# Gate and value products of two units by seven block products for eight, in a kernel of chunk-selected attention and a gated feed-forward

## The chip, the cores and the metric

The kernel runs on one core of a Trainium2 chip. The metric is the device time in microseconds. A core has five engines with a queue each that run side by side and wait for each other by semaphores: TensorE (PE, matmuls, written to the eight banks of PSUM; its weight loads are shown as PEld), VectorE (DVE), ScalarE (ACT), GpSimd (POOL) and SyncE (SP, which here issues most DMA transfers). Each queue is worked off in order.

## The reference

The inputs are q, k and v of 4 batches, 8 heads, 768 positions and 64 dimensions in float32. Keys are seen in 24 chunks of 32. For each query an upper bound of its score in each chunk is formed from the chunk's smallest and largest keys, and the six chunks with the largest bounds are kept. Attention runs over the kept chunks under a causal mask. Its output, with the heads side by side, is a matrix x of 3072 x 512, which goes through a gated feed-forward:

```
ub = sum(max(q * k_min, q * k_max))              # per query and chunk, -1e9 where not causal
sel = the 6 chunks with the largest ub
attn = softmax(where(sel and causal, scale * q @ k.T, -1e9))
x = (attn @ v), heads side by side               # 3072 x 512
out = (sigmoid(x @ w_gate) * (x @ w_val)) @ w_out   # 512 -> 1536 -> 512
```

## The kernel before

The 3072 rows are cut into eight units of 384 (three blocks of 128 positions each). Unit 0 holds first blocks, where nothing has to be selected; units 1 to 7 hold the others. The unit list names them `u0` to `u7`.

For each unit the keys and queries are turned and cast (`prepare`, `keys_wide`, `keys_blocks`, `turn_queries`), then `choose` makes the bounds (`ub`, TensorE), turns them (`ubn`, VectorE), takes the eight largest (`mx`), compares (`ap`), turns the result back (`apt`) and copies it as a mask beside the queries (`hqm`). `attend` makes scores (`sc`, TensorE, line L1064), exponentials (`exp`, ScalarE, L1075), the causal cut (`cm`, GpSimd, L1081), the products with v (`pv`, TensorE, L1097), and scales and turns the result (`rz`, `x`, `xps`, `xT`; L1114 to L1124 and the copies at L575 and L577). So `xT` of a unit is the turned 512 x 384 input of its feed-forward, as four slices of 128 x 384 in float16.

`ffn` (L1131 and after) works on one unit. For each of the 12 blocks `fb` of 128 hidden columns it makes the gate product `g` (four matmuls of 128 x 128 weights with 128 x 384 inputs, added up in one PSUM bank; L1147), `tanh` of half of it on ScalarE (L1155), the value product `v` (four matmuls, L1147), and on VectorE `hg` = (tanh + 1) * v (L1159); the factor 1/2 is put in at the end. Then `o` multiplies the 12 `hg` with w_out for each of the three row blocks, in three parts `o0`, `o1`, `o2` of four matmuls (L1172), `osb` copies the bank (L1181), and `out` stores it.

The weights w_gate, w_val and w_out come by nine transfers that GpSimd issues (`wg0` to `wo2`, L719 to L725); SP issues the loads of q, k and v and the stores.

No operation is emitted where it stands in the code. Each is added to a `Plan` with its engines, its inputs and outputs, its buffers and a priority. Buffers come in kinds with a number of slots (`ps` are the eight PSUM banks). `Plan.order` then walks through all operations with a cost model, and picks at each step an operation, an engine and buffer slots; a list of nudges and a list of landing times of the transfers steer it. The result is the order in which the operations are emitted, and so the order of each engine's queue.

Of the kernel before, what the change touches and what calls it, by code (L numbers as in the profile page):

```python
# [17 lines left out]
HOP = {PE: 60, ACT: 40, DVE: 40, POOL: 70, SP: 30}  # L18
FAR = float("inf")
STEP, PHASE, AWAKE = 3413.0, 300.0, 0.58  # L20
SHARED = {128: (0.145, 0.95), 256: (0.173, 0.90), 512: (0.22, 0.83), 768: (0.29, 0.78), 2048: (0.5, 0.5)}
SENT, LANDED = {SP: 700, POOL: 2700}, 1100
# [12 lines left out]
class Op:  # L35
    def __init__(self, name, engines, emit, prio, dma, rows, port):
        self.name, self.engines, self.emit, self.prio, self.dma = name, engines, emit, prio, dma
        self.rows, self.port = rows, port
        self.deps = []
        self.bufs = []  # L40
        self.start = self.done = self.engine = None


class Clock:


    def __init__(self):
        self.full = {}
        self.busy = {}

    def rate(self, t):
        w = int((t - PHASE) // STEP)
        if w not in self.full:
            self.full[w] = self.busy.get(w - 1, 0.0) >= AWAKE * STEP
        return self.full[w]

    def took(self, s, busy):
        t, left = s, busy
        while left > 1e-6:
            slow = 1.0 if self.rate(t) else 1.9  # L60
            w = int((t - PHASE) // STEP)
            edge = PHASE + (w + 1) * STEP
            step = min(left * slow, edge - t)
            self.busy[w] = self.busy.get(w, 0.0) + step
            left -= step / slow
            t += step
            if edge - t < 1e-6:
                t = edge
        return t - s


class Plan:

# [36 lines left out]
    def walk(self, land, prio=None, script=None, slow=1.0):  # L110

        free = {e: 0.0 for e in HOP}
        slots = {k: [[0.0, None] for _ in range(n)] for k, n in self.slots.items()}
        line = {SP: 0.0, POOL: 0.0}
        port = {DVE: 0.0, POOL: 0.0}
        flight = []
        clock = Clock()
        left, until, seen = {}, {}, {}
        out = []

        def inputs(op, e):
            t = 0.0
            for d, raw in op.deps:
                if raw is None:
                    t = max(t, d.start)
                elif d.dma is None and d.engine == e:
                    if raw and e != PE:
                        t = max(t, d.done + 25)
                else:
                    t = max(t, d.done + HOP[e])  # L130
            for b in op.bufs:
                if b.kind == "ps":
                    for (other, r), done in seen.get(b, {}).items():
                        if other != e and r in op.rows:
                            t = max(t, done + HOP[e])
            if e == POOL:
                t = max(t, port[DVE])
            elif e == DVE and op.port:
                t = max(t, port[POOL])
            return t  # L140

        def room(op):
            t = 0.0
            if script is not None:
                for b in op.bufs:
                    if b not in left:
                        t = max(t, slots[b.kind][b.slot][0])
                return t
            need = {}
            for b in op.bufs:  # L150
# [3 lines left out]
            for (kind, cat), bs in need.items():  # L154
                kinds[kind] = kinds.get(kind, 0) + len(bs)
                if (kind, cat) in self.caps:
                    mine = sorted(s[0] for s in slots[kind] if s[1] is not None and s[1].cat == cat)
                    over = len(mine) + len(bs) - self.caps[kind, cat]
                    if over > 0:
                        t = max(t, mine[over - 1])  # L160
# [143 lines left out]
NUDGES = """  # L304
# [1007 lines left out]
```

## Time and profile before

| what | value |
|---|---|
| time, median of 3 runs | 293.85 us (293.5 to 294.12) |
| span of the profiled execution | 292.8 us |
| timed median less that span | 1.05 us |
| PE busy | 277.3 us, 95% |
| DVE busy | 188.2 us, 64% |
| ACT busy | 195.5 us, 67% |
| POOL busy | 91.8 us, 31% |
| granted TensorE clock, mean | 0.988 |
| `g` and `v` matmuls (L1147), all units | 384 each, 79.1 and 78.8 us busy |
| `hg` on DVE (L1159) | 96, 545 ns mean |
| `tanh` on ACT (L1155) | 96, 496 ns mean |

The profile is one execution of the program; its span reaches from the first to the last instruction. "Busy" is the union of an engine's instructions, so a mean duration times a count is more than the busy time where instructions overlap. The windows view gives the busy time of each engine in a stretch, with the number of instructions in brackets and the granted TensorE clock. The waits view tells for each engine what ended its idle time: microseconds in total, times, the longest.

### The profile page before, as it was taken

To read this page: it belongs to the slowest core of one execution; us is meant where nothing else is said; L and a number is where in the kernel's file an instruction comes from. 1 tells how busy PE (TensorE), PEld (TensorE's weight loads), DVE (VectorE), ACT (ScalarE), POOL (GpSimd) and SP (SyncE) were. 2 spreads that over 40 slices of the span, in tenths; PEclk is the share of its full clock that TensorE was granted. 3 is DMA by queue.
4 is the path that set the end of the run, shared out by engine and by line. 5 is a ranking of instruction groups with operands and counts; after the bars stand their busy time and mean duration, and the time that the engine had idled before them with its cause. 6 is when DMAs were issued, how large, how long until landed. Compare 5 with 4: busy or idle time off the path is not lost.

```text
span 292.8 us, 6981 instructions
## 1 busy us (share of the span) xinstructions
PE 277.3 (95%) x2668; PEld 177.3 (61%) x2668; DVE 188.2 (64%) x560; ACT 195.5 (67%) x399; POOL 91.8 (31%) x162
## 2 busy tenths in 40 slices
PE   2769998999999999999999999999999999999995
PEld 2545655767664566556666668676566556655653
DVE  8276883996999289999899999654134124423420
ACT  7575747977984879458889998877464466332321
POOL 5663304934652337013336864212000011000000
PEclk9977999999999999999999999999999999999999
DMA  7999999999968999499995300001100020002002
GB/s 164 213 251 223 197 199 241 216 143 172 182 101 90 201 168 191 82 209 169 152 211 124 113 3 3 0 2 39 72 2 1 36 74 0 2 36 74 0 2 107
DMA packets 123377, 32.69 MB, mean 112 GB/s; under 512 B 111440, under 2 KB 120400, under 8 KB 123344
## 3 DMA queue, kind: packets, MB, share of 16 engines
q1 hardware_dynamic: 118592, 27.53, 53.3%
q0 software_dynamic: 4752, 4.72, 9.5%
q8 instruction: 21, 0.34, 0.5%
q14 instruction: 12, 0.10, 0.1%
HBM read 30.67 MB, written 6.29 MB: 126 GB/s over the span
## 4 chain that ended last, share of the span: by engine, by line
PE 73%; DMA 12%; DVE 6%; SPq 3%; POOL 2%; issue 1%; ACT 0%; DVEq 0%; ACTq 0%
PE o_u L1172 20%; PE g_u L1147 16%; PE v_u L1147 16%; PE sc_u L1064 10%; DMA wo<-in_moe_w_out_dram 8%; PE pv_u L1097 6%; SPq L743 2%; DMA kq_u<-in_k_dram 2%; PE ube_u L1003 2%; DMA k<-in_k_dram 2%; PE xps_u L1124 2%; DVE kcr L788 1%; DVE kt L954 1%; DVE kx L788 1%; SPq L738 1%
## 5 line engine op out<-in xcount | busy, mean ns | idle before, releaser
L1075 ACT ACTIVATE att_u<-sc_u 128x512 f16<-128x512 f32 (+3 forms) x184 | 88.1, 550 | 14.3 <-PE sc_u L1064 13.6
L1159 DVE SCALAR_TENSOR_TENSOR hg_u<-gate_u,v_u 128x384 f16<-128x384 f16 x96 | 51.9, 545 | 53.6 <-PE v_u L1147 36.7
L1147 PE MATMUL g_u<-xT_u,wg 128*128 128x384 f16 x384 | 79.1, 329 | 0.0
L1147 PE MATMUL v_u<-xT_u,wv 128*128 128x384 f16 x384 | 78.8, 328 | 0.2 <-DMA wv<-in_moe_w_val_dram 0.2
L1155 ACT ACTIVATE gate_u<-g_u 128x384 f16<-128x384 f32 x96 | 47.6, 496 | 38.6 <-DVE hg_u L1159 21.5
L1172 PE MATMUL o_u<-wo,hg_u 128*128 128x512 f16 (+1 forms) x288 | 67.4, 377 | 1.3 <-DMA wo<-in_moe_w_out_dram 1.3
L1081 POOL TENSOR_SCALAR_AFFINE_SELECT att_u<-att_u 128x384 f16<-128x384 f16 (+1 forms) x56 | 28.2, 509 | 102.5 <-ACT att_u L1075 101.7
L1147 PEld LDWEIGHTS <-wv 128*128 128x128 f16 x384 | 36.7, 98 | 23.2 <-DMA wv<-in_moe_w_val_dram 0.6
L1147 PEld LDWEIGHTS <-wg 128*128 128x128 f16 x384 | 36.5, 99 | 21.7 <-issue 1.5
L1172 PEld LDWEIGHTS <-hg_u 128*128 128x128 f16 x300 | 27.9, 98 | 28.5 <-issue 1.7
L1181 ACT ACTIVATE osb_u<-o_u 128x512 f32<-128x512 f32 (+1 forms) x20 | 12.0, 598 | 26.1 <-PE o_u L1172 24.4
L1097 PEld LDWEIGHTS <-att_u 128*128 128x128 f16 x640 | 25.5, 98 | 4.7
L1097 PE MATMUL pv_u<-v,att_u 128*128 128x65 f16 x640 | 27.9, 193 | 0.0
L1064 PE MATMUL sc_u<-hqo,hko 128*128 128x128 f16 (+2 forms) x220 | 27.8, 243 | 0.1
L1064 PE MATMUL sc_u<-hqe,hke 128*128 128x128 f16 (+2 forms) x220 | 27.1, 243 | 0.2 <-ACT att_u L1075 0.2
L1064 PEld LDWEIGHTS <-hke 128*128 128x128 f16 x220 | 16.8, 98 | 5.7 <-issue 1.2
L1064 PEld LDWEIGHTS <-hko 128*128 128x128 f16 x220 | 16.2, 98 | 4.8 <-issue 0.2
L780 POOL CAST v<-v 128x512 f16<-128x512 f32 x23 | 13.9, 617 | 16.8 <-DMA v<-in_v_dram 16.6
L577 DVE COPY xT_u<-xps_u 128x384 f16<-128x384 f16 (+1 forms) x17 | 5.8, 339 | 14.4 <-PE xps_u L1124 14.3
L1116 DVE TENSOR_TENSOR x_u<-pv_u,rz_u 128x384 f16<-128x384 f32 (+1 forms) x28 | 14.5, 524 | 0.4
L1026 DVE MAX8 mx_u<-ubn_u 128x8 f32<-128x8 f32 (+16 forms) x152 | 12.4, 158 | 0.1
L788 DVE TRANSPOSE_TENSOR_REDUCE kcr<-k 128x24 f32<-128x768 f32 x12 | 11.3, 944 | 0.3 <-DMA k<-in_k_dram 0.3
(121 smaller groups left out, 306.1 us busy)
## 6 DMA issues: line engine op xcount, KB each, us to landing
v<-in_v_dram SPq DMA_DIRECT2D x23, 256.0 KB, 5.4
out_dram<-osb_u SPq DMA_DIRECT2D x23, 256.0 KB, 2.5
k<-in_k_dram SPq DMA_DIRECT2D x12, 384.0 KB, 6.0
q<-in_q_dram SPq DMA_DIRECT2D x12, 384.0 KB, 6.5
wg<-in_moe_w_gate_dram POOLq DMA_DIRECT2D x3, 512.0 KB, 9.5
wv<-in_moe_w_val_dram POOLq DMA_DIRECT2D x3, 512.0 KB, 11.5
wo<-in_moe_w_out_dram POOLq DMA_DIRECT2D x3, 512.0 KB, 21.9
kf<-in_k_dram SPq DMA_DIRECT2D x8, 128.0 KB, 3.9
```

The source lines that it names most:

```text
L780: plan.add(f"v16_{b}_{ib}", {POOL: pool(H * D)}, lambda e: nc.gpsimd.tensor_copy(v16[b % 2][:, ib, :, 0:D], at(t)), reads=[t], writes=[("v ...
L788: plan.add(f"kx{m}_{name}_{p}", {DVE: dve(size)}, lambda e, m=m, op=op: nc.vector.tensor_reduce(out=outs[m](), in_=src(), op=op, axis=AX.X ...
L1026: nc.vector.max(at(mx)[:, e_, j, :], at(ubn)[:, e_, j, 0:max(8, u.seen[j])])
L1064: nc.tensor.matmul(at(t)[:, o:o + 128 * m], hk[b % 2][e_][:, p, 128 * jb:128 * jb + 128], hq[u.side][e_][:, p, 128 * x:128 * (x + m)], sta ...
L1075: plan.add(f"exp_{u.name}_{h}_{y}", {ACT: act(n)}, lambda e, t=t, att=att, b0=b0, n=n: nc.scalar.activation(at(att)[:, b0:b0 + n], at(t), ...
L1081: nc.gpsimd.affine_select(out=dv, in_=dv, compare_op=ALU.is_ge, fill=0.0, base=0, pattern=[[0, u.m], [1, 128]], channel_multiplier=-1)
L1097: nc.tensor.matmul(at(pv)[:, last, x, :], at(att)[:, c:c + 128], v16[b % 2][:, jb, h, :], start=(jb == 0), stop=(jb == ib))
L1116: plan.add(f"x_{u.name}_{p}", {DVE: dve(u.t)}, lambda e: nc.vector.tensor_tensor(at(x_).rearrange("p a (e d) -> p e a d", e=2), at(pv)[:, ...
L1147: nc.tensor.matmul(at(t), w16[:, c, 128 * fb:128 * fb + 128], at(u.xt)[:, c, :], start=(c == 0), stop=(c == 3))
L1155: plan.add(f"tanh_{u.name}_{fb}", {ACT: act(T)}, lambda e, g=g, gate=gate: nc.scalar.activation(at(gate), at(g), AF.Tanh, scale=0.5), read ...
L1159: plan.add(f"hg_{u.name}_{fb}", {DVE: dve(T)}, lambda e, w_=w_, gate=gate, hg=hg: nc.vector.scalar_tensor_tensor(at(hg), at(gate), 1.0, at ...
L1172: nc.tensor.matmul(at(o), at(hgs[fc])[:, 128 * tb:128 * tb + 128], wo16[:, fc, lo:hi], start=(fc == 0), stop=(fc == NFB - 1))
```

## The change

For units 5 and 6, `ffn` is replaced by `ffn_pair`, which takes both at once. The weights of gate and of value are seen as 2 x 2 blocks (halves of the 512 inputs by halves of the 1536 hidden columns), the two units' inputs as 2 x 2 blocks (halves of the inputs by unit). The 2 x 2 product of blocks takes seven products for eight, with sums of blocks in their place. For each of six pairs of hidden blocks `f` and `f + 6`, and for gate and value each, there are seven products `P1` to `P7` of two matmuls, in three PSUM banks (`su`, `sq`, `sr`), three copies `E0`, `E1`, `E3` of partial results to SBUF in float32 and three adds `C0`, `C1`, `C3`. `tanh` and `hg` then read three of the four results from SBUF and one from PSUM.

The sums of weight blocks (`Sg0` to `Sg3`, `Sv0` to `Sv3`) are made once, 128 x 1536 in float16, the sums of inputs (`T0` to `T3`) once, 128 x 768 in float16.

The projection of all units is now made by `project_out`, with the same matmuls; for the pair the order in which the 12 parts are added is another. Unit 7's `xT` takes a slot of the kind `qf`, since units 5 and 6 hold both slots of `xt` at once.

The cost model, the nudges and the landing times are gone. `ORDER` is a table of 1782 words, one for each operation in the order of emission, with an engine where it is not the first one allowed and with the buffer slots. The table is another order for all units, not for units 5 and 6 alone. In it the selection and the first scores of unit 7 come ahead of those of unit 6, and units 5 and 6 reach their products together, before unit 7's first.

```diff
-    def walk(self, land, prio=None, script=None, slow=1.0):
...
+    def order(self):
+        ops = {op.name: op for op in self.ops}
+        out = []
+        for word in ORDER.split():
+            name, _, slots = word.partition(":")
+            name, _, engine = name.partition("@")
+            op = ops.pop(name)
+            op.engine = engine or next(iter(op.engines))
+            fresh = [b for b in op.bufs if b.slot is None]
+            for b, slot in zip(fresh, slots.split(",") if slots else (), strict=True):
+                b.slot = int(slot)
             out.append(op)
...
+ORDER = """
+vf1_3:0 kf0_0:0 v10 ap0 vf1_2:1 ident hq1 kf1_0 epat0:0 vf1_1:2 qf0_0:1 ident16 v11 hq0 epat kcr0 qf1_0 ap1 kcr1
...
+qf0_u7_2 v16_3_4 exp_u5_0_1 Sv0@DVE:0 g_u4_0:2,0,12 qm_u7_2@ACT sc_u5_2_2:0,3 osb_u3_2@DVE cm_u5_1 sc_u5_0_2:5
...
+    def mixed(w16, name, key, prio, raw):
...
+        for i, x, op, y, need in ((0, a21, ALU.add, a22, []), (1, s(0), ALU.subtract, a11, [(t, 0)]),
+                                  (2, a11, ALU.subtract, a21, []), (3, a12, ALU.subtract, s(1), [(t, 1)])):
+            op = plan.add(f"S{name}{i}", {POOL: pool(n), DVE: dve(n, 2)}, lambda e, i=i, x=x, op=op, y=y: (
+                nc.vector if e == DVE else nc.gpsimd).tensor_tensor(at(t)[:, i], x(), y(), op),
...
+    def ffn_pair(ua, ub_, base, span):
...
+        for i, x, op, y, need in ((0, b12, ALU.subtract, b11, ka[0:2] + kb[0:2]), (1, b22, ALU.subtract, tt(0), kb[2:4] + [(ts, 0)]),
+                                  (2, b22, ALU.subtract, b12, kb), (3, b21, ALU.subtract, tt(1), ka[2:4] + [(ts, 1)])):
...
+                op = mul(1, u_, True)
...
+                keep_(0, u_)
+                mul(2, q_, True)
+                add(0, q_)
+                mul(5, r_, True)
+                keep_(3, r_)
+                use(0)
+                mul(6, u_, False)
+                keep_(1, u_)
+                mul(3, r_, False)
+                add(1, r_)
+                use(1)
+                mul(7, u_, False)
+                add(3, u_)
+                use(3)
+                mul(4, u_, False)
+                use(2)
...
-    ffn(units[5], 6.0, 0.95)
...
+    mix = {"g": mixed(wg16, "g", "wg", 5.4, k3), "v": mixed(wv16, "v", "wv", 5.6, q3)}
     attend(units[6], 6.0)
-    ffn(units[6], 7.0, 0.95)
+    ffn_pair(units[5], units[6], 6.4, 1.6)
```

Here `mul` is a product of two matmuls, `keep_` a copy `E`, `add` an add `C`, and `use` a `tanh` for the gate or an `hg` for the value. So in the bank `su` the products 1, 6, 7 and 4 are added up one after the other, and what stands in it is read (`E0`, `E1`, `C3`) before the next product adds to it.

## The prediction

> **What bounds the kernel now.** I read the page's shares first, then the windows, the waits of TensorE, and the timeline of the stretch that the change replaces.
>
> ```profile
> span 292.8 us, 6981 instructions
> ...
> PE 277.3 (95%) x2668; PEld 177.3 (61%) x2668; DVE 188.2 (64%) x560; ACT 195.5 (67%) x399; POOL 91.8 (31%) x162
> ```
>
> ```profile
> core 0: us, PE busy (x) PEld busy (x) DVE busy (x) ACT busy (x) POOL busy (x), PEclk, DMA share, GB/s
> 0.00:20.00 20.00, 10.24 (x83) 7.54 (x83) 12.29 (x33) 13.88 (x22) 11.75 (x26) 0.96 1.05 202
> 20.00:40.00 20.00, 19.85 (x140) 11.62 (x139) 14.59 (x50) 11.49 (x26) 7.13 (x12) 0.87 1.21 215
> ...
> 160.00:180.00 20.00, 20.00 (x316) 13.64 (x314) 18.66 (x77) 18.41 (x37) 13.37 (x23) 1.00 0.19 54
> 180.00:200.00 20.00, 20.00 (x237) 14.57 (x235) 13.30 (x40) 15.85 (x34) 5.08 (x9) 1.00 0.01 2
> 200.00:220.00 20.00, 20.00 (x166) 12.16 (x164) 5.47 (x13) 12.01 (x26) 2.57 (x5) 1.00 0.11 41
> 220.00:240.00 20.00, 20.00 (x146) 11.62 (x144) 4.99 (x10) 9.72 (x19) 1.04 (x2) 1.00 0.11 41
> 240.00:260.00 20.00, 20.00 (x192) 12.88 (x190) 8.48 (x18) 9.14 (x20) 1.01 (x2) 1.00 0.00 1
> ```
>
> From 100 us to 280 us TensorE is busy all the time at clock 1.00. Its 12.3 us of idleness lie before 100 us (the five windows there hold 87.7 of 100 us). VectorE is nearly full from 120 to 180 us (18.7 to 19.0 of 20) and a quarter full after 200 us, where the products of units 5 and 6 stand. A busy TensorE need not be at its peak, so I look at the spacing.
>
> ```profile
> 216.43 0.81 PE L1147 MATMUL g_u<-xT_u,wg 128*128 128x384 f16 x4
> ...
> 217.08 0.81 PE L1147 MATMUL v_u<-xT_u,wv 128*128 128x384 f16 x4
> ...
> 217.73 0.81 PE L1147 MATMUL g_u<-xT_u,wg 128*128 128x384 f16 x4
> ```
>
> Four matmuls start every 0.65 us, 0.1625 us each; nothing else stands between them. So a matmul taken away here is worth 0.1625 us, as long as TensorE still finds its inputs ready.
>
> **What is removed.** Units 5 and 6 now take 2 x 12 x 2 products of four matmuls: 48 x 0.65 = 31.2 us. The change takes 2 x 6 x 7 products of two matmuls: 84 x 0.325 = 27.3 us. It saves 24 matmuls (and 24 weight loads, which lie beside them: PEld is 61% busy), 3.9 us of TensorE. All other TensorE work is the same, in another order.
>
> **What is added, and its price.** VectorE gets 36 adds `C`, 8 copies `E`, 7 of the weight sums `S` (128x1536) and 4 activation sums `T` (128x768). ScalarE gets 28 copies `E`, GpSimd one `S`. The 24 `tanh` and 24 `hg` stay.
>
> ```profile
> 184.61 0.56 DVE L1116 TENSOR_TENSOR x_u<-pv_u,rz_u 128x384 f16<-128x384 f32 x1
> 185.08 0.54 DVE L1159 SCALAR_TENSOR_TENSOR hg_u<-gate_u,v_u 128x384 f16<-128x384 f16 x1
> 185.54 0.57 DVE L1037 STREAM_TRANSPOSE apt_u<-ap 128x384 f16<-128x384 f16 x1
> ```
>
> Back to back, a 128x384 operation of VectorE takes 0.47 us of it; alone, it lasts 0.55. That is the price of `C`, `E` and `hg`. No row shows a 16-bit sum of two SBUF tensors. Nearest from below: the f16 copy of 64x1536 at 0.55. From above, four times 0.47 = 1.88 for 1536 elements at one per cycle. I take a middle row, 16-bit data that come through one port: the f16 copy `xT_u` takes 0.286 for 256 and 0.358 for 384 elements, 0.072 per 128 more, so 1.0 us for `S` and 0.57 for `T`.
>
> ```profile
> L577 DVE COPY xT_u<-xps_u x17: 248/358/358, 56.1 to 265.4; 128x384 f16<-128x384 f16 x15, 128x256 f16<-128x256 f16 x2
> L577 DVE COPY xT_u<-xpsf x6: 280/286/292, 16.5 to 69.6; 128x256 f16<-128x256 f16 x6
> L577 DVE COPY hke<-epat x3: 547/547/555, 5.7 to 6.6; 64x1536 f16<-64x1536 f16 x3
> ```
>
> The Trainium skill, VectorE: DVE Perf Modes, section "The perf-mode tier table", says that such a sum of two 16-bit SBUF tensors runs at two elements per cycle; by its breakdown an estimate for `S` would be 0.95 us, and the sum below would stand. At the one element per cycle of this case's two-source rows it would go to the slower rival.
>
> **Where it lies: three stretches of the table.** I add the operations of each stretch by their row prices.
>
> (1) From `Sv0` to `o0_u4_0`, where the eight `S` are put among unit 4's products and the selection of units 7 and 6. TensorE: 28.5 us. VectorE without `S`: 12 `hg` and 4 `x` at 0.47 (7.5), 4 each of `ubn` and `apt` at 0.5 (4.0), 4 `mx` at 1.0 (4.0), 4 `ap` at 0.4 (1.6), 7 `hqm` at 0.36 (2.5), small ones 3: 22.6. With 7 `S` at 1.0: 29.6, 1 us more than TensorE has. With the lower price 26.5, with the upper 35.8. This is the part of the trace where VectorE is full already, and it is in order: `hqm` of unit 6 is queued behind all `S`, and unit 6's scores behind it. I take 0.5 us lost, half of the excess, because the last of the stretch's operations are not all waited for at once.
>
> Another cost is in this stretch. `ap` reads two SBUF tensors, and lasts 0.84 us where GpSimd worked beside it (its cast at 172.32 lasted 0.82), 0.46 where it did not:
>
> ```profile
> 172.61 0.84 DVE L1031 TENSOR_TENSOR ap<-ubn_u,mx_u 128x288 f16<-128x288 f32 x1
> 175.78 0.46 DVE L1031 TENSOR_TENSOR ap<-ubn_u,mx_u 128x288 f16<-128x288 f32 x1
> ```
>
> `S` reads two as well. GpSimd works some 9 of 28 us here, so a third of the 7 meet it: 7/3 x 0.4 = 0.9 us at most. It is within the excess that I only half count, and goes to the range. The Trainium skill, SBUF — State Buffer, section "Who interferes with whom", has this as a rule against the change: a sum with both inputs in SBUF waits for a GpSimd instruction that reads SBUF; were all seven hit, it would be 2.8 us of VectorE for the 0.9, and the sum up to 1.9 us worse.
>
> (2) From `P1g_u5u6_0` to `g_u7_0`: TensorE 18.9 us (51 half products, 16.6, and 2.3 of unit 7's attention). VectorE: 22 `C`, 9 `hg`, 5 `E`, 2 `x`, 38 x 0.47 + 0.5 = 18.4 us, 97%. If each operation took its lone 0.55: 21.4, 2.5 more than TensorE has. Within one group the bank `su` goes to and fro: four products and three reads of it, 4 x 0.325 + 3 x (0.5 + some 0.25 of matmul end and hand-over) = 3.5 us, against 2.3 us that TensorE works for the group. So two or three groups must interleave, as the table has them, and what covers one group's wait is another's products. I take 1.4 us lost, between 0 and 2.5: no engine that is 97% full and waits at each step keeps the other one full.
>
> (3) From `g_u7_0` to `g_u7_4`: TensorE 19.8 us, VectorE 35 x 0.47 = 16.5 (lone: 19.3). No loss taken. Before (2), VectorE has 4 of 16.7 us to do, then the `T`: 4 x 0.57 ahead of `P1g`, beside 4.4 us of TensorE: covered; at 0.94 each it would stand out by nothing to 1 us. ScalarE stays under 80% in (2) and (3). After `g_u7_4` come 28.5 us of TensorE with 4 us of VectorE.
>
> **The front.** Its operations are the same, their order isn't. The second key half is now SP's second transfer and no longer the third (one step, 0.55 us earlier; the first transpose waits for it), `hkf1` and `hkp111` (0.6 and 1.5 us) stand ahead of `wg0` on GpSimd, `vf_0` goes from fifth to fourteenth on SP, and `vc_2` moves to GpSimd. All nine weight loads keep their order, and the last one, `wo2`, still holds unit 0's projection:
>
> ```profile
> PE o_u L1172 <- DMA wo<-in_moe_w_out_dram: 1.3, 1, 1.3
> ```
>
> TensorE has 28.0 us of work ahead of that wait in both orders, so `wo2` ties the two together: without it up to 1.3 us could go, and a start later by 1.5 would shift everything. I take 0, with -1.3 to +1.5 in the range.
>
> **Sum.** The profiled execution has a span of 292.8 us; the timed median is 293.85, 1.05 more. 292.8 - 3.9 + 0.5 + 1.4 = 290.8, and with the 1.05: **291.9 us**.
>
> **Rivals.** *VectorE becomes the bound* (slower). Place: stretch (1). If `S` runs at one element per cycle (1.88), VectorE has 35.8 us to TensorE's 28.5; 7.3 lost for 0.5, so 298.7. It decides from the point where the losses pass 3.9 us: `S` over some 1.2 us each, with 1.4 lost in (2). Half of it: 295.0. For it: VectorE's 18.7 of 20 us there, and the two-source rows. Against: the 16-bit rows. *The work is hidden fully*: nothing lost in (1) and (2), 290.0; with the front's 1.3 gained, 288.7. For it: in 120 to 180 us VectorE is 94% full and TensorE has no wait. Against: there it is not waited for at each step. *The losses eat the saving*: both upper ends, 1.0 + 2.5, and the saving is 0.4: 293.4. *No matmul is saved*: the loops say 168 for 192 and the rest is untouched; I give it nothing.
>
> **Chances.** The forecast (290.6 to 293.2): 0.56. Hidden fully, or a gain in front: 0.14. Losses eat it, within 0.6 us of before: 0.10. VectorE the bound, or the front later: 0.20. About 0.2% (0.6 us) is what a measurement of this kernel can tell from no change. So faster 0.70, same 0.10, slower 0.20. The range goes from 289.4 (nearly all hidden) to 295.2 (into the slower rival).
>
> **What would show it.** Some 2644 matmuls for 2668. The rows of `S` near 1.0 us and of `T` near 0.57. TensorE's waits after 150 us, now none, some 2 us, most of them for `C` and `E` between 215 and 240 us. I am wrong if `S` lasts 1.8, if VectorE has no gap in (1) while TensorE has several us, if TensorE has no waits in (2), or if unit 1's first product starts over 1 us off its 64.4 us.

## The result, and the profile after

The change made the kernel slower. Four runs gave a median of 297.54 us (297.31 to 299.27), four runs of the kernel before beside them 293.99 (293.5 to 294.53); the ratio is 1.0136, 95% interval 1.0105 to 1.0166. The forecast was 291.9 us, with a range from 289.4 to 295.2.

The page of the kernel after, its span and its busy times:

```profile
span 295.6 us, 7004 instructions
...
PE 274.8 (93%) x2644; PEld 175.3 (59%) x2644; DVE 221.1 (75%) x620; ACT 203.9 (69%) x423; POOL 99.1 (34%) x162
```

The 24 matmuls are gone (2644 for 2668), and TensorE is busy 2.5 us less; yet the span is 2.8 us longer. The profiled execution took 297.33 us, 1.7 more than its span. In every later run of the kernel before, too, the time is 1.65 to 1.79 us above the span of the same execution. So the profile of before, 292.8 us, is that of an execution of some 294.5 us (an estimate), and the 1.05 us of the prediction were the median less the span of another, slower execution; the forecast, built on the median, is not moved by that. The medians are 3.55 us apart, the two profiled spans 2.8, and these 2.8 are what is explained here.

The waits of TensorE, after (us in total, times, longest):

```profile
PE pvf L618 <- POOL attf L611: 4.9, 3, 4.2
PE kfT L567 <- DMA kf<-in_k_dram: 4.3, 1, 4.3
PE v_u L898 <- DVE ubn_u L765: 2.5, 1, 2.5
PE o_u L929 <- DMA wo<-in_moe_w_out_dram: 1.2, 1, 1.2
```

Before, the row of `pvf` was

```profile
PE pvf L867 <- POOL attf L860: 1.4, 2, 1.0
```

and there was none of a `v` for `ubn`. So two waits are new: 4.2 us ahead of a `pvf` of the front's third block, and 2.5 us of a `v` for `ubn`, in the stretch where the weight sums stand. The second shows in the windows (busy us of TensorE, its weight loads, VectorE, ScalarE, GpSimd; then granted clock and DMA):

```profile
160.00:180.00 20.00, 20.00 (x242) 12.96 (x239) 19.13 (x38) 17.78 (x32) 13.71 (x18) 1.00 0.24 68
180.00:200.00 20.00, 17.50 (x261) 12.41 (x252) 19.78 (x88) 14.46 (x31) 6.38 (x8) 1.00 0.01 2
200.00:220.00 20.00, 19.96 (x280) 14.67 (x278) 7.86 (x21) 16.95 (x36) 4.67 (x9) 1.00 0.09 32
220.00:240.00 20.00, 19.45 (x190) 12.45 (x187) 18.47 (x39) 17.02 (x40) 1.83 (x3) 1.00 0.03 11
```

To see where the 2.8 us come from I use one measure throughout. For a product, add up the full-rate time of all TensorE work that is queued ahead of it (0.65 us for four 128x384 matmuls, 0.325 for two, and so on), and take that from its start time: this is TensorE's *lag* there. Only changes of the lag are used; it grows where TensorE waits or runs slowly.

| first matmul of | before: start, lag | after: start, lag |
|---|---|---|
| unit 0's first gate product `g_u0_0` | 22.01, 16.30 | 24.61, 19.24 |
| the last part of its first projection `o2_u0_0` | 48.21, 20.21 | 50.42, 22.42 |
| unit 1's first gate product `g_u1_0` | 64.40, 21.04 | 66.73, 23.48 |
| unit 4's fourth gate product `g_u4_3` | 179.88, 23.00 | 175.10, 25.29 |
| unit 4's first projection, last part `o2_u4_0` | 201.36, 23.06 | 204.63, 28.11 |
| unit 7's first gate product `g_u7_0` | 266.05, 23.21 | 243.87, 29.88 |
| the last projection `o2_u7_2` | 288.13, 23.22 | 290.91, 29.90 |

At the end the lag is 6.7 us larger, and 3.9 us of work are saved: 2.8. Of the 6.7 us, 2.3 are there before unit 4 starts (**the front**), 2.8 are lost among unit 4's products (**stretch 1**), 1.6 from there to `g_u7_0`, nearly all of it among the block products (**stretch 2**), and nothing after that.

Stretch 1 in detail. The timeline of VectorE, after (start, duration, line, operation):

```profile
178.15 0.94 DVE L958 TENSOR_TENSOR Sg<-wg,Sg 128x1536 f16<-128x1536 f16 x1
179.02 0.54 DVE L910 SCALAR_TENSOR_TENSOR hg_u<-gate_u,v_u 128x384 f16<-128x384 f16 x1
179.49 3.39 DVE L958 TENSOR_TENSOR Sg<-wg 128x1536 f16<-128x1536 f16 x1
182.80 1.27 DVE L958 TENSOR_TENSOR Sv<-wv,Sv 128x1536 f16<-128x1536 f16 x1
183.99 0.57 DVE L765 STREAM_TRANSPOSE ubn_u<-ube_u 128x384 f32<-128x384 f32 x1
```

And GpSimd's row in the same microseconds:

```profile
178.12 3.94 POOL L958 TENSOR_TENSOR Sv<-wv 128x1536 f16<-128x1536 f16 x1
```

The third weight sum of the gate, `Sg2`, lasts 3.39 us where the sum ahead of it lasts 0.94. While GpSimd makes `Sv2` (178.12 to 182.06), VectorE's sum does not get on; it ends 0.8 us after GpSimd's. Behind it in VectorE's queue stand `Sv3` and the two `ubn` of unit 7, which empty PSUM banks that `v_u4_5` needs. So TensorE stands still from 182.1 to 184.6 us.

The front. GpSimd's timeline, after:

```profile
20.04 0.62 POOL L330 CAST vf<-vf 128x512 f16<-128x512 f32 x1 [5.50 <-DMA vf<-in_v_dram]
20.61 1.23 POOL L611 TENSOR_SCALAR_AFFINE_SELECT attf<-attf 128x512 f16<-128x512 f16 x2
21.78 0.77 POOL L470 DMA_DIRECT2D wg<-in_moe_w_gate_dram  x1
```

The cast `vc_2` waits 5.5 us for `vf_2`, which was issued at 9.8 us, after `wg0` and `wv0` (8.6 and 9.5 us), and landed at 20.0; before, it was issued at 9.7, ahead of them, and landed at 13.9. Behind `vc_2` stand the causal cut and the issue of the other seven weight loads: `wg1` is issued at 21.8 us for 18.4, and `wo2` lands at 50.4 for 48.2. `o2_u0_0` starts as `wo2` lands, in both kernels.

### The profile page after: what moved, and what is told of

Read it like the earlier page. It is cut to its first block, busy times and chain, and to the rows that moved or that the text cites. A ratio compares the mean times of both kernels' runs of the same rounds, so it can differ in the third digit from the quotient of the medians.

```text
span 295.6 us, 7004 instructions
## 1 busy us (share of the span) xinstructions
PE 274.8 (93%) x2644; PEld 175.3 (59%) x2644; DVE 221.1 (75%) x620; ACT 203.9 (69%) x423; POOL 99.1 (34%) x162
## 4 chain that ended last, share of the span: by engine, by line
PE 58%; DMA 15%; DVE 14%; ACT 6%; POOL 2%; issue 2%; SPq 1%; DVEq 0%; POOLq 0%; ACTq 0%
PE o_u L929 17%; PE v_u L898 9%; PE g_u L898 8%; DMA wo<-in_moe_w_out_dram 8%; PE sc_u L815 7%; PE pv_u L848 4%; DMA k<-in_k_dram 4%; DMA vf<-in_v_dram 3%; ACT att_u L826 3%; PE suv_u5u L1009 2%; PE sug_u5u L1009 2%; PE ube_u L754 2%; DVE Sg L958 2%; DVE kcr L539 1%; PE srv_u5u L1009 1%
## 5 line engine op out<-in xcount | busy, mean ns | idle before, releaser
L826 ACT ACTIVATE att_u<-sc_u 128x512 f16<-128x512 f32 (+2 forms) x184 | 88.0, 562 | 10.6 <-PE sc_u L815 10.1
L898 PE MATMUL v_u<-xT_u,wv 128*128 128x384 f16 x288 | 58.9, 327 | 2.5 <-DVE ubn_u L765 2.5
L929 PE MATMUL o_u<-wo,hg_u 128*128 128x512 f16 (+1 forms) x252 | 59.1, 376 | 1.2 <-DMA wo<-in_moe_w_out_dram 1.2
L898 PE MATMUL g_u<-xT_u,wg 128*128 128x384 f16 x288 | 59.3, 329 | 0.2 <-ACT gate_u L906 0.2
L910 DVE SCALAR_TENSOR_TENSOR hg_u<-gate_u,v_u 128x384 f16<-128x384 f16 x72 | 38.4, 539 | 27.6 <-PE v_u L898 20.2
L906 ACT ACTIVATE gate_u<-g_u 128x384 f16<-128x384 f32 x72 | 35.9, 502 | 21.2 <-PE g_u L898 16.0
L898 PEld LDWEIGHTS <-wv 128*128 128x128 f16 x288 | 27.9, 98 | 19.5 <-issue 3.6
L898 PEld LDWEIGHTS <-wg 128*128 128x128 f16 x288 | 27.6, 98 | 17.3 <-issue 1.3
L865 DVE RECIPROCAL rz_u<-pv_u 128x6 f32<-128x6 f32 (+1 forms) x28 | 5.0, 179 | 10.0 <-PE pv_u L848 9.8
L539 DVE TRANSPOSE_TENSOR_REDUCE kx<-k 128x24 f32<-128x768 f32 x12 | 11.3, 952 | 0.9 <-DMA out_dram<-osb_u 0.9
```

Of the source, the lines that this page charges most:

```text
L539: plan.add(f"kx{m}_{name}_{p}", {DVE: dve(size)}, lambda e, m=m, op=op: nc.vector.tensor_reduce(out=outs[m](), in_=src(), op=op, axis=AX.X ...
L826: plan.add(f"exp_{u.name}_{h}_{y}", {ACT: act(n)}, lambda e, t=t, att=att, b0=b0, n=n: nc.scalar.activation(at(att)[:, b0:b0 + n], at(t), ...
L898: nc.tensor.matmul(at(t), w16[:, c, 128 * fb:128 * fb + 128], at(u.xt)[:, c, :], start=(c == 0), stop=(c == 3))
L906: plan.add(f"tanh_{u.name}_{fb}", {ACT: act(T)}, lambda e, g=g, gate=gate: nc.scalar.activation(at(gate), at(g), AF.Tanh, scale=0.5), read ...
L910: plan.add(f"hg_{u.name}_{fb}", {DVE: dve(T)}, lambda e, w_=w_, gate=gate, hg=hg: nc.vector.scalar_tensor_tensor(at(hg), at(gate), 1.0, at ...
L929: nc.tensor.matmul(at(o), hgs[c][1][1]()[:, 128 * tb:128 * tb + 128], wo16[:, fc, lo:hi], start=(c == 0), stop=(c == NFB - 1))
```

## The experiments

Every kernel below is the one after with the words of its table, and in three runs lines of code, edited as shown; the ratio is to the kernel before, timed beside it (its median was 293.99 us beside the kernel after, 294.7 to 295.1 beside the others). Lags are from the profiled execution of each.

| run | edit | ratio (95%) | lag at `g_u1_0` | lag added in stretch 1 | lag at `o2_u7_2` |
|---|---|---|---|---|---|
| after | | 1.0136 (1.0105 to 1.0166) | 23.48 | 2.82 | 29.90 |
| `s1_sv2_dve` | `Sv2` on VectorE | 1.0037 (1.0014 to 1.0060) | 23.15 | 0.48 | 27.21 |
| `s2_late` | all `S` later, on VectorE | 1.0047 (1.0025 to 1.0069) | 24.10 | 0.16 | 28.87 |
| `f1_vc2` | `vc_2` on ScalarE | 1.0109 (1.0070 to 1.0148) | 21.11 | 4.48 | 29.09 |
| `f3_weights_later` | `wg0`, `wv0` later | 1.0085 (1.0053 to 1.0117) | 22.29 | 4.49 | 30.79 |
| `c1_both` | `vc_2` and `Sv2` moved | 0.9985 (0.9965 to 1.0005) | 23.43 | 0.48 | 27.78 |
| `s3_sv2_alone` | `Sv2` on GpSimd, later | 0.9980 (0.9958 to 1.0002) | 22.76 | 0.23 | 26.49 |
| `h1_gates_first` | front in another order | 0.9933 (0.9911 to 0.9956) | 21.38 | 0.16 | 25.56 |

(Stretch 1 is from `g_u4_3` to `o2_u4_0`.)

**Does GpSimd's sum hold VectorE's?** One word of the table.

```diff
-ubn1_u7 Sv2 v_u4_5:6
+ubn1_u7 Sv2@DVE v_u4_5:6
```

> Only edit to the changed kernel: the weight sum Sv2 runs on VectorE and no longer on GpSimd, at its place in the table. Theory, two engines with two SBUF inputs each slow each other: Sg2 takes some 1.0 us for the 3.39 us it took beside Sv2, Sv2 takes 1.0 us, VectorE is 1.4 us less busy there, ubn of unit 7 comes 1.5 to 2.5 us earlier, and the time falls by 1.5 to 2.5 us from 297.5, to 295 to 296. Rival, VectorE is simply over-full in this stretch: a whole sum more on it makes it worse, the time goes up by 0.5 to 1 us.

Measured: 1.0037, so 0.0099 less than the 1.0136 of the kernel after; of 294 us that is 2.9 us, some 1.1 either way by the two intervals. The rows of VectorE's timeline in this run:

```profile
179.12 0.94 DVE L957 TENSOR_TENSOR Sg<-wg 128x1536 f16<-128x1536 f16 x1
179.99 0.94 DVE L957 TENSOR_TENSOR Sv<-wv,Sv 128x1536 f16<-128x1536 f16 x1
...
181.82 0.90 DVE L957 TENSOR_TENSOR Sv<-wv 128x1536 f16<-128x1536 f16 x1
```

`Sg2` is back at 0.94 us, and all eight sums on one engine lose TensorE 0.48 us for 2.82. The meeting of the two sums is the cause in stretch 1, and VectorE, with one sum more, is not over-full.

```diff
-o1_u4_0 exp_u6_5_0 ... o2_u4_0 exp_u7_7_2 ... osb_u4_0 pv_u7_7 ...
+o1_u4_0 Sg0@DVE:1 exp_u6_5_0 ... o2_u4_0 Sg1@DVE exp_u7_7_2 ... osb_u4_0 Sg2@DVE pv_u7_7 ...
```

(and so on, one sum after each of unit 4's projection parts and stores).

> Only edit to the changed kernel: all eight weight sums run on VectorE after unit 4's first projection part (near 198 us) and before T0, where VectorE has little to do, and no longer among unit 4's gate and value products. If the sums cost the 2.75 us that TensorE falls back between unit 4's fourth product and its projection, all of it comes back: 297.5 falls to some 294.8, and VectorE in the 20 us from 200 us on is some 8 us busier. If something else in that stretch of the new order costs it (the two selections of units 7 and 6 side by side), TensorE falls back there as before and the time stays within 1 us of 297.5.

Measured: 1.0047. Stretch 1 loses 0.16 us, so nothing else in it was wrong; but 0.76 us are lost afterwards, between `o2_u4_0` and `o2_u4_2`, where the sums now stand. The kernel is no better than the one-word edit: the place of the sums hardly matters, the company they keep does, by 2.3 us.

```diff
-cm_u6_5 o2_u4_0
+cm_u6_5 Sv2 o2_u4_0
```

(on top of `vc_2` on ScalarE, so beside the run with both edits below.)

> Both edits, but Sv2 is on GpSimd again and stands after the cut cm of unit 6's sixth head, near 200 us, where no weight sum runs on VectorE. It measures the price of the sum on GpSimd by itself. If the 3.94 us of the changed kernel were the meeting with VectorE's sum, it takes some 1.5 to 2 us here; if GpSimd is that slow by itself, 3 us or more. TensorE has scores and projections to do beside it, so the time should be that of the kernel with both edits, or up to 0.4 us less, since VectorE has a sum less in unit 4's stretch.

Measured: 0.9980. The group of the sum in this run (count, busy us, mean ns):

```profile
L957 POOL TENSOR_TENSOR Sv<-wv 128x1536 f16<-128x1536 f16 x1 | 3.1, 3099 | 0.0
```

I expected 1.5 to 2 us if the 3.94 were due to the meeting; it is 3.10. So GpSimd is slow by itself, over three times VectorE's 0.94. Every profile repeats this: 3.94 us in the three kernels where the sums meet (after, `f1_vc2`, `f3_weights_later`), 3.09 to 3.10 in the six where `Sv2` is alone on GpSimd. The 0.84 us more in the kernel after are about what VectorE's `Sg3` (0.94 us, undisturbed) took beside its first microsecond. So the times fit two sums that do not share: `Sv2` waited for `Sg3`, and then `Sg2` for `Sv2`. (Their starts, 178.12 and 178.15 us, are too close to say which of the first two was issued first.)

The Trainium skill, SBUF — State Buffer, section "Who interferes with whom", says that issue order decides who blocks, and speaks of an exclusive lock. These rows agree: one sum at full speed, the other standing still.

**What is late in the front?**

```diff
-xpsf_1_0:2 vc_2 rzf_0_0:0 ... xf_0_1:0 kn_u1_1:5
+xpsf_1_0:2 rzf_0_0:0 ... xf_0_1:0 vc_2@ACT kn_u1_1:5
```

> Only edit to the changed kernel: the cast vc_2 goes from GpSimd to ScalarE, just ahead of kn_u1_1, so that GpSimd's queue (cmf_2, then wg1 to wo2) no longer stands behind the wait for vf_2. Theory 1, GpSimd's queue: wg1 is issued some 4 us earlier than 21.8 us, wo2 lands near 48 us for 50.4, unit 0's first projection part o2 and unit 1's first product (66.7 us) come 1 to 2 us earlier, and the time falls from 297.5 to some 296 us. Theory 2, the traffic itself: the weights that are issued earlier take the bandwidth from vf_2 and unit 1's keys, TensorE's first gate product moves later than 24.6 us, and the time stays at 297.5 or goes up by as much as a microsecond.

Measured: `wg1` issued at 16.9 us for 21.8, `wo2` landed at 46.6, unit 1's first product at 64.35 us for 66.73, and unit 4's fourth gate product starts with the lag of before (22.82, before 23.00). So in this profile the whole 2.3 us of the front are gone. Other profiles show less: over the eight kernels with `vc_2` on ScalarE and the weights where they were, unit 1's first product starts at 64.35 to 67.07 us, 65.9 on average; over the three with it on GpSimd at 66.40 to 67.34, 66.8 on average. And the time fell by only 0.0027, 0.8 us with some 1.4 either way, so it is not told apart from no change. In the profile stretch 1 lost 4.48 us for 2.82. The windows of this run there:

```profile
180.00:182.00 2.00, 0.00 (x0) 0.00 (x0) 2.00 (x3) 0.68 (x2) 0.54 (x1) 1.00 0.02 4
182.00:184.00 2.00, 1.88 (x9) 1.03 (x9) 2.00 (x16) 0.00 (x0) 0.00 (x0) 0.75 0.00 0
184.00:186.00 2.00, 2.00 (x12) 1.25 (x10) 1.24 (x3) 1.93 (x4) 0.56 (x1) 0.50 0.00 0
186.00:188.00 2.00, 2.00 (x12) 1.14 (x11) 1.26 (x4) 0.86 (x3) 0.79 (x2) 0.90 0.00 0
```

The pause made by `Sv2` is the same 2.5 us, but here the granted clock falls to 0.50 after it, for 3.4 us in all; that costs 1.7 us. In the profile of the kernel after, with a pause as long, the clock stayed at 1.00:

```profile
180.00:182.00 2.00, 2.00 (x34) 1.30 (x25) 2.00 (x1) 1.53 (x4) 2.00 (x1) 1.00 0.00 0
182.00:184.00 2.00, 0.11 (x1) 0.00 (x0) 2.00 (x3) 1.16 (x3) 0.90 (x2) 1.00 0.00 0
184.00:186.00 2.00, 1.39 (x9) 0.86 (x9) 2.00 (x16) 0.00 (x0) 0.00 (x0) 1.00 0.00 0
```

What differs is where the pause lies. In every trace the recorded changes of the clock lie whole multiples of 3.41 us apart (here 25.98, 182.99 and 186.41 us). Laid on that grid, the pause of this run falls whole into one step (2.49 us idle in the step that ends at 182.99); that of the run `f3_weights_later`, where the clock fell too, nearly so (2.25); that of the kernel after is split (1.5 and 1.0). These are three cases, and no run was made to test it. So whether the clock falls is a matter of the single execution: by the mean clock it fell in two of this kernel's four timed runs (0.994) and in one of the four of the kernel after. Nor do the four times here follow it: 296.67 and 298.46 us with the fall, 296.79 and 298.18 without. So the slow clock explains this profile, not the small gain in time.

```diff
-vf_0:1 hkp010 kfT_1:5 qf16_1:5 wg0 wv0 kf16_1:6 ... cmf_0_1 k1_u1:0
+vf_0:1 hkp010 kfT_1:5 qf16_1:5 kf16_1:6 ... cmf_0_1 wg0 wv0 k1_u1:0
```

> Only edit to the changed kernel: GpSimd issues wg0 and wv0 after the two causal cuts of the first block and no longer ahead of them, near 11.5 and 12.3 us for 8.6 and 9.5. Theory 2, the traffic: vf_2 and unit 1's keys, issued from 9.8 us on, no longer stand behind 1 MB of weights; vf_2 lands near 14 us for 20.0, the first gate product starts near 22 us for 24.6, wo2 lands near 48 us, and the time falls by some 2.2 us to 295.3. Theory 1, GpSimd's queue alone: vf_2 early helps in the same way. A third theory, that the front is late for the order of TensorE's own work: vf_2 lands early, but the first gate product stays at 24 us or more and the time within 0.5 us of 297.5.

Measured: 1.0085. `vf_2` landed at 13.7 us as expected. TensorE's timeline:

```profile
19.71 0.82 PE L897 MATMUL g_u<-xT_u,wg 128*128 128x384 f16 x4 [0.30 <-DMA wg<-in_moe_w_gate_dram]
24.80 1.46 PE L897 MATMUL v_u<-xT_u,wv 128*128 128x384 f16 x4 [4.26 <-DMA wv<-in_moe_w_val_dram]
```

The first gate product is 4.9 us earlier; then the first value product waits 4.26 us for `wv0`, and unit 0's fourth gate product starts at 29.93 us, where it was (29.83). So the late `vf_2` is the weights' traffic, and whichever of the two is put first, the other is late. Unit 1's first product gained 1.2 us, since `wo2` landed at 49.2. Here too the clock fell in stretch 1 (4.49 us lost).

Both one-word edits, `Sv2@DVE` and `vc_2@ACT`:

> Both one-word edits to the changed kernel at once: vc_2 on ScalarE, ahead of kn_u1_1, and Sv2 on VectorE. Alone, the first made TensorE 2.5 us earlier up to unit 4, and then lost 4.5 us in unit 4's stretch, with a granted clock of 0.50 from 184 to 186 us; the second lost only 0.5 us there. Theory: the two causes are independent, and the slow clock came from the stall that Sv2 made; then unit 4 starts with a lag of 22.8 us, 0.5 is lost in its stretch and 1.7 among the block products, the span is some 290.8 us, 2.1 below the second edit alone, and the time some 2 us below the kernel before. Rival: unit 4's stretch waits for something whose time is fixed (the loads of k, q and v for the last units), so TensorE that comes earlier only waits longer there, and the time stays at that of the second edit alone.

Measured: 0.9985, 0.0052 (1.5 us) below the run with `Sv2` on VectorE alone. Stretch 1 lost 0.48 us and the clock stayed at 1.00 there, and none of the ten timed runs of this kernel, nor of the ten of `s1_sv2_dve`, has a mean clock below 0.998: without the pause the clock did not fall in this stretch. But the span was 293.5 us and not 290.8: in this profile the front gained nothing (23.43 at `g_u1_0`). TensorE's timeline, first of the run with `vc_2` alone, then of this one:

```profile
23.22 1.49 PE L897 MATMUL g_u<-xT_u,wg 128*128 128x384 f16 x4
24.50 1.49 PE L897 MATMUL v_u<-xT_u,wv 128*128 128x384 f16 x4
25.78 0.92 PE L897 MATMUL g_u<-xT_u,wg 128*128 128x384 f16 x4
26.53 0.49 PE L652 MATMUL kT_u<-ident,kn_u 128*128 128x128 f32 x3
```

```profile
24.39 1.49 PE L897 MATMUL g_u<-xT_u,wg 128*128 128x384 f16 x4
25.67 1.49 PE L897 MATMUL v_u<-xT_u,wv 128*128 128x384 f16 x4
26.95 1.49 PE L897 MATMUL g_u<-xT_u,wg 128*128 128x384 f16 x4
28.23 0.85 PE L652 MATMUL kT_u<-ident,kn_u 128*128 128x128 f32 x3
```

Four matmuls that last 1.49 us together run at half rate, 0.81 is full rate. The half rate is older than the pause ahead of `vf_2`: in both, four `pvf` already last 0.40 us at 13.4 us, and 0.29 where the record of the clock gives full rate (first row the run with `vc_2` alone, second `h1_gates_first` below, which is at full rate from 14.83 to 18.24 us):

```profile
13.42 0.40 PE L617 MATMUL pvf<-vf,attf 128*128 128x65 f16 x4 [0.47 <-POOL attf L610]
16.87 0.29 PE L617 MATMUL pvf<-vf,attf 128*128 128x65 f16 x4
```

(The windows give 1.00 for these microseconds all the same, since the record of the clock begins with its first change.) Half rate ends at 25.98 us in the one and at 29.49 us in the other, with the same front; and `vf_2` landed at 18.8 us in the one and at 20.0 in the other. So a single profile is good to some 1 to 2 us in the front, and the timed ratio is what counts. The Trainium skill, TensorE: Matmul & The Clock Gate, section "Part 1: The HAM clock gate", has a free-running window of some 3.4 us behind the clock; the steps of 3.41 us between its changes agree with it.

A milder form, `wv0` alone after the two cuts (on top of the run `e2_spread` below):

> As the run before it here, and GpSimd issues wv0 after the two causal cuts of the first block, near 11.5 us for 9.5, so that vf_2 and unit 1's keys stand behind one weight transfer and not two. If the 4 us in which TensorE stands still before 21 us are the traffic's, vf_2 lands near 16 us for 20, wv0 near 22 us, the fourth gate product of unit 0 starts 1 us or more earlier, wo2 stays at 46.5 to 48 us, and the time falls by some 1 us below the run before it, to 0.99 to 0.995 of the kernel before. If wv0 is what the second product then waits for, nothing is gained.

Measured: 1.0004 (0.9976 to 1.0033), and 1.0019 (0.9998 to 1.0041) without it: not told apart. `vf_2` landed at 19.5 us; one weight transfer ahead of it is enough.

**What is the pair worth, and what the order?** Units 5 and 6 with `ffn`, twelve gate and twelve value products of four matmuls each, in the new order with `vc_2` on ScalarE; no sums, `E` or `C`.

```diff
-    ffn_pair(units[5], units[6], 6.4, 1.6)
+    ffn(units[5], 6.2, 0.95)
+    ffn(units[6], 7.0, 0.95)
```

> The new order without the block products: vc_2 on ScalarE as in the run with both edits, units 5 and 6 with the twelve gate and twelve value products of four matmuls each, no weight sums and no sums of inputs; unit 5's and unit 6's products stand where the block products stood, with unit 7's attention between them, and unit 7's after them. 2668 matmuls for 2644. If the block products save their 3.9 us less the losses found so far (0.5 in unit 4's stretch, 1.7 among them), this kernel takes 1.7 us more than the one with both edits, 292.5 us of span, near the kernel before. If the block products are worth nothing, it takes the same as the one with both edits or less. If the order itself is slower, it is more than 1 us above the kernel before.

Measured: 1.0214, no fair answer: my placing of unit 7's attention lost 5.2 us. So once more, with that attention spread out:

> Again the new order without the block products (four matmuls each for units 5 and 6, no sums), with unit 7's attention spread over all of unit 5's and half of unit 6's products; the first try lost 5.2 us from 216 us on, most of it at 235 to 245 us, where the end of unit 7's attention stood together and the granted clock fell after it. With under 1 us lost from 216 us on, its span is that of the run with both edits (293.5) plus 3.9 of matmuls, less the 0.5 lost in unit 4's stretch and the 1.7 among the block products: some 295. So the pair would be worth 1.7 us at equal front. If it comes out at 293.5 or less, the block products are worth nothing here.

Measured: 1.0041 (1.0009 to 1.0073), span 295.5. It loses 0.5 us from `o2_u4_2` on. In the same front the pair is worth 1.0041 less 0.9985, 0.0056 or 1.6 us, with some 0.004 either way from the two intervals; the expectation, from its losses, was 1.7. This is against one order of the eight products, placed by hand; with another that loses nothing the pair would be worth some 0.5 us less. And this order without the pair is itself slower than before, by 1.2 us with `vc_2` moved.

**What is lost among the block products?** First, four of VectorE's eight copies to ScalarE (on top of both edits).

```diff
-E3v_u5u6_0@DVE:6 ... E0v_u5u6_2@DVE:4 ... E3g_u5u6_5@DVE:6 ... E3v_u5u6_4@DVE:1
+E3v_u5u6_0:6 ... E0v_u5u6_2:4 ... E3g_u5u6_5:6 ... E3v_u5u6_4:1
```

> Both edits, and four of VectorE's eight copies E (E3v of pair 0, E0v of pair 2, E3g of pair 5, E3v of pair 4) on ScalarE, which is 68% busy there. Theory, VectorE's 97% is what costs the 1.7 us among the block products: with some 2 us less for it, the loss falls under 1 us, and the time by 0.7 us or more against the kernel with both edits. Rival, the hand-over in the banks is what costs it (a product waits for the hg that reads the bank's last result, and too few products stand between): the loss stays at 1.7 us within 0.3.

Measured: 0.9991 (0.9970 to 1.0013). The loss from `o2_u4_2` to `g_u7_0` is 1.96 us, it was 1.69. Only two of the four copies stand ahead of `g_u7_0`, so from the first `P1g` to there VectorE is busy 18.3 of 20.6 us for 19.3 of 20.3, and not 2 us less. This microsecond, at least, gained nothing. More than half of the loss (0.9 us) is at one place. TensorE's timeline in the run with `Sv2` alone on GpSimd, and VectorE's `hg` that it waits for:

```profile
230.47 0.48 PE L1008 MATMUL suv_u5u<-T_u5u,wv 128*128 128x384 f16 x2
231.87 0.48 PE L1008 MATMUL suv_u5u<-xT_u,wv 128*128 128x384 f16 x2 [0.45 <-DVE hg_u L1038]
```

```profile
231.27 0.55 DVE L1038 SCALAR_TENSOR_TENSOR hg_u<-gate_u5u,suv_u5u 128x384 f16<-128x384 f16 x1
```

`P4v` of pair 0 ends its bank at 230.9 us, `hg` reads it from 231.27 to 231.82, and `P1v` of pair 2 takes the bank at 231.87. VectorE works without a gap from 229.87 to 232.29 us, so part of this is its queue. So I put `sc_u7_2_1` and `P1g` of pair 3 ahead of `P1v`:

```diff
-P1v_u5u6_2:1 tanh_u5u6_0_7:2 sc_u7_2_1:6 E0v_u5u6_2@DVE:4 P3g_u5u6_3 tanh_u5u6_1_2:1 P1g_u5u6_3:2,0,1,4
+tanh_u5u6_0_7:2 sc_u7_2_1:6 P1g_u5u6_3:2,0,1,4 P1v_u5u6_2:1 E0v_u5u6_2@DVE:4 P3g_u5u6_3 tanh_u5u6_1_2:1
```

> As the run with Sv2 alone on GpSimd, and among the block products unit 7's scores sc_u7_2_1 and the product P1g of pair 3 stand ahead of P1v of pair 2, which waits for the hg that reads the bank's last result. Theory, the hand-over in the banks: half a microsecond of other work now lies under that wait, the 0.9 us lost there becomes some 0.4, and the 1.7 us lost among the block products some 1.2; the time falls by 0.5 us. Rival, VectorE full: hg comes when VectorE's queue lets it, the products that were moved ahead make no difference, and the 1.7 us stay.

Measured: 1.0019 (0.9998 to 1.0041), and 2.8 us lost for 1.7. `P1g` had to wait for its own bank, until a `tanh` had read it, and `P1v` now waited behind it. That `tanh` was late because the one ahead of it on ScalarE waited 1.6 us for a buffer. So with five buffers for three:

```diff
-gates[c] = g = Buf("gate" if c < 2 else "kt", f"gate_{tag}_{x}_{fb}", [128, T], F16)
+gates[c] = g = Buf("gate" if c < 2 else "kx" if (x, fb) in GATES else "kt", f"gate_{tag}_{x}_{fb}", [128, T], F16)
```

> As the run in which sc_u7_2_1 and P1g of pair 3 were moved ahead, and the tanh results of the third and fourth of the four partial results of a gate (c = 2 and 3) take turns over five buffers (three of the kind kt, two of the kind kx, idle by then) and no longer over three. In that run, and in the changed kernel, ScalarE stood still for 1.6 us near 230 us, with its tanh waiting for the hg that still reads the buffer, and P1g of pair 3 then waited for the next tanh to read its bank. Theory, buffers: with five, this wait of 1.6 us is gone, the bank of P1g of pair 3 is free before 231 us, and the loss among the block products falls from 2.8 us to about 1 us, below the 1.7 of the table's own order; the time falls by some 1.5 us against that run and comes to 0.995 of the kernel before. Rival, VectorE: it works without a gap from 228 to 232 us, so hg comes no earlier, and 1.7 us or more stay lost.

Measured: 1.0014 (0.9988 to 1.0040), 2.5 us lost. The wait for the buffer is gone, the loss is not:

```profile
231.38 0.48 ACT L327 COPY c3g_u5u<-srg_u5u 128x384 f32<-128x384 f32 x1 [1.29 <-PE srg_u5u L1010]
231.76 0.50 ACT L1035 ACTIVATE gate_u5u<-sug_u5u 128x384 f16<-128x384 f32 x1
```

The `tanh` that frees the bank stands behind a copy `E3g`, which waits 1.29 us for its product. Three edits, none a gain, and in all three the loss was 1.7 us or more, as the rivals named before the runs had it. The rows show the hand-over of banks between three queues that are each in order; whether VectorE's full queue or the banks cost the time is not told apart. The table's own order was the best of the four, and which order would do without the loss stays open.

**A front without the pause.** `wg0` and `wv0` after the two cuts again, and unit 0's gate products ahead of its value products, since they need only `wg0` (on top of `s3_sv2_alone`).

```diff
-g_u0_0:0,0,0 ... v_u0_0:3 ... g_u0_1:7,1,1 hg_u0_0 wo2 kT_u1_0:6 tanh_u0_1 v_u0_1:5 ... g_u0_2:1,2,2 ... g_u0_3:2,3,3
+g_u0_0:0,0,0 ... g_u0_1:7,1,1 tanh_u0_0 g_u0_2:1,2,2 tanh_u0_1 kT_u1_0:6 g_u0_3:2,3,3 v_u0_0:3 ... v_u0_1:5
```

> As the run with Sv2 alone on GpSimd, and wg0 and wv0 are issued after the first block's two causal cuts (so vf_2 is not behind them), and unit 0's second, third and fourth gate products, which need only wg0, stand ahead of its first value product, which needs wv0. With this place of the weights alone, vf_2 landed at 13.7 us, the first gate product started at 19.7 us, and TensorE then waited 4.3 us for wv0. Theory, the pause for vf_2 and the slow clock after it are what is left of the front's loss: TensorE works through the gate products in that wait, unit 0's fifth gate product starts 2 us or more earlier, and unit 1's first product comes as early as wo2 lets it (49 us for its start of projection, so 0.5 to 1 us earlier); the time falls to some 0.995 of the kernel before. Rival, the weights' stream is what bounds it: wo2 lands at 49 us and nothing is gained.

Measured: 293.35 us median (292.03 to 294.43), 0.9933 (0.9911 to 0.9956): faster than both kernels, by 2.0 us and by 6 us. TensorE's timeline:

```profile
20.68 4.05 PE L897 MATMUL g_u<-xT_u,wg 128*128 128x384 f16 x12
25.12 0.81 PE L897 MATMUL g_u<-xT_u,wg 128*128 128x384 f16 x4
```

The first three gate products (twelve matmuls, at half rate) and the fourth fill what was a wait of 4.26 us. `o2_u0_0` starts at 48.32 us, as `wo2` lands (48.3): now the weights' stream is the bound, as it was before. Against the run `s3_sv2_alone` this front is worth 0.0047, 1.4 us with some 0.9 either way.

> As the run before it here, and the loads of v_0_2, v_0_3 and unit 2's keys and queries wait until v16_0_1 has been made (v_0_2 takes the buffer of v_0_1), near 38 us, so that they do not share the stream with the weights. If the stream bounds the front, wo2 lands 1.5 to 3 us earlier than in the run before, unit 0's last projection part and unit 1's first product come 1.5 us or more earlier than there, and the time falls to some 0.99 of the kernel before. If unit 1's values or unit 2's keys are then what comes too late, TensorE falls back between 48 and 65 us and the time does not fall.

Measured: 0.9948 (0.9923 to 0.9974), not told apart from the run before it. `wo2` landed 2.1 us earlier (46.2) and `o2_u0_0` started 0.9 us earlier, but the lag then grew by 1.8 us up to `g_u1_0` (1.1 without the hold), so 0.2 us were left there. The stream is not the only bound any more; the waits named there are for unit 1's values (0.5 us), which the edit holds back, and its scores (0.3).

## Why the prediction was wrong, step by step

Two terms of the sum failed: the meeting of `S` with GpSimd in stretch (1), put at 0.9 us at most and within the excess, cost 2.3; and the front, put at 0, cost 2.3.

- **Saving** (3.9 us, 24 matmuls): right. The queued work is 262.3 us for 266.2, and the pair is worth 1.6 us in the same front (1.7 by 3.9 less the losses, 0.5 and 1.7).
- **Prices**: right where I gave one. `S` on VectorE took 0.94 to 1.27 us (1.0 forecast), save the one that met GpSimd's, `T` 0.55 to 0.87 (0.57), `C` 0.55 alone and 0.47 back to back. The one sum on GpSimd got no price at all. That is the first fault.
- **Stretch 1** (0.5 us lost): the excess was right, 0.48 us with all sums on VectorE. The term for the collision, "0.9 at most", was worked out with GpSimd's operations of before, 0.5 to 0.8 us each, as if only those could be met. The change itself puts an operation of 3.9 us there, and the next `S` of VectorE beside it: 2.3 us. The rule on such meetings was cited there, and the price put on seven meetings with short operations and not on the one long one.
- **Stretch 2** (1.4, 0 to 2.5): 1.6. Right in size and place. VectorE was 95% busy there (97% forecast). Of the two reasons given, a full VectorE and a bank that goes to and fro, neither is shown to be the one: 1 us less on VectorE left the loss, and the rows at the place where most of it lies show both.
- **Stretch 3** and after: nothing lost, right.
- **The front** (0, from -1.3 to +1.5): 2.3 us late. I listed that `vc_2` moves to GpSimd and that the weight loads keep their order, and did not ask who stands behind `vc_2` in that queue: seven weight loads. I saw that `wo2` ties both orders, which held, and took its landing for fixed, which it was not: 50.4 for 48.2. Nor did I put a price on `vf_2`, which is issued 0.1 us later and lands 6.1 us later, since `wg0` and `wv0` now go ahead of it. In timed runs the first of the two is worth 1.5 us (1.0037 less 0.9985) and the second, with the gate products put first, 1.4 (0.9980 less 0.9933); how the 2.3 us of the one profile divide between them is not shown.
- **Rivals**: "VectorE becomes the bound" named the right stretch and the right sign, with 298.7 and 295.0, but by a price of `S` that was not so. The two mis-sized terms were never added to each other (293.4 for the upper ends of the stretches, and the front's +1.5 apart), but even their sum, 294.9, lies below the 297.5 that were measured: each upper end was too low.
- **What would show it**: two of the four signs of being wrong were met. Unit 1's first product was 2.3 us off its 64.4. VectorE had next to no gap from 180 to 200 us (19.78 of 20) while TensorE had 2.5. As forecast, TensorE lost 1.6 us among the block products (the waits view names only 0.4 of it, the lag shows the rest), and `S` did not last 1.8, save the one of 3.39.

Sum with the measured terms: -3.9 + 0.5 + 2.3 + 1.6 + 2.3 = 2.8, the difference of the spans.

What each part is worth in timed runs, of 294 us: the two sums that meet 2.9 us (1.0136 less 1.0037); `vc_2` in GpSimd's queue 1.5 us (1.0037 less 0.9985); the pair -1.6 us (0.9985 less 1.0041); the rest of the new order 1.2 us (1.0041). Together 4.0 us, the 1.0136; each has about 1 us either way.

## What to carry to other kernels

An operation that a change adds has to be priced on the engine it runs on, and then as company for what runs beside it: a slow operation on an engine that is 34% busy cost more than seven fast ones on one that is full. Where an operation changes its queue, ask what it waits for there and list everything behind it, transfers above all; a wait of one cast held seven weight loads. When a fix gains less than its stage shows, the granted clock behind the next stall can explain that in one profile; whether it explains the time is read from the clocks of all timed runs, and here it did not.

## What the runs showed of the hardware

- A 16-bit sum of two 128x1536 SBUF tensors took VectorE 0.94 us and GpSimd 3.10; where they met, VectorE's took 3.39 and GpSimd's 3.94 (three kernels), as if the one that came second stood still until the other was done.
- After a pause of TensorE of 2.5 us the granted clock fell to 0.50 for 3.4 us in two profiles (`vc_2` moved, weights later) and stayed at 1.00 in that of the kernel after, which had the same pause. In every trace the changes of the clock lie whole multiples of 3.41 us apart; the pause lay in one such step in the first two, and across two steps in the third.
- TensorE started at half rate (four `pvf` in 0.40 us for 0.29). In the profiles with the pause ahead of `vf_2` and no earlier change of the clock it stayed there until 26.0 to 29.7 us. The windows view gives 1.00 for that time, since the record of the clock begins with its first change.
- A transfer of 256 KB (`vf_2`) landed 3.7 to 4.2 us after its issue with no weight transfer ahead of it (four kernels), and 9.0 to 11.0 us after it with one or two ahead (twelve).
